# K's later rests and copies queued behind a unit, the first weight conversions spaced out, layer 2's blocks split one block further ahead

## Chip, core and metric

One Trainium2 chip, one core. The metric is the device time of one execution in microseconds (us): the median over several runs. Everything runs on the five engines of that core: TensorE (PE in the rows, with PEld for its weight loads), VectorE (DVE), ScalarE (ACT), GpSimd (POOL) and SyncE (SP, which here only issues DMAs).

## What is computed

Three stages follow one another; the output of each is the input of the next.

```python
# attention: 2 batches, 8 heads, 768 rows, 64 columns a head
q_bucket, k_bucket = hash6(q @ proj), hash6(k @ proj)      # 6 sign bits each
scores = where(q_bucket == k_bucket, scale * q @ k.T, -1e9)
attn = softmax(scores) @ v
x = attn as 1536 tokens x 512
x = (silu(x @ w_gate) * (x @ w_val)) @ w_out              # layer 1, 512 -> 1536 -> 512
h = x @ w_in                                              # layer 2, 512 -> 2048 -> 512
out = (max(h, 0) + alpha * min(h, 0)) @ w_out2
```

## The kernel before

**Attention.** Two heads make a pair, four pairs make the 512 columns of a token. An item is one pair with 256 query rows, a unit is one head of an item. The items run in a fixed order: items 0 to 7 are the four pairs with the first 512 query rows (items 0 and 1 are pair 0, 2 and 3 pair 1, 4 and 5 pair 2, 6 and 7 pair 3), and the rest follow. A unit passes through `banks` (three score tiles S, a copy `se` of each on ACT, running maxima `m` on DVE), `top` (transposes `mt` on PE, row maximum `mq` on DVE), `back` (transposes `mb`, the subtraction `s_sub` of L333 on DVE, the exponential `s_exp` of L338 on ACT) and `values` (matmuls `po`, then the division on DVE, a rounded copy `xh` on ACT and its rest `xl` on POOL). Eight steps of the generator `attention()` make a unit. Several units are in flight, a stage apart.

**K of a pair.** Products run in a reduced format on PE, so an operand is held as a rounded part and a rest. For K of a pair, `load_k` (L165) loads the plain rows into `nat`, on SP, and the rounded part into the tile `kt`, on POOL's queue. `rest_k` (L177) subtracts the two: head 0 on POOL, head 1 on DVE. `copy_k` (L181) copies the rounded part to a second half on ACT, once per head. Then `hash_k` makes the hash rows from both (matmuls `hp`, `mk` on DVE, L210 on ACT). For items 2, 4 and 6 these calls stand in `prep`, which is written two items ahead of its use.

**Weights.** A block is 128 x 512. Its raw 64-bit words are loaded (`raw_load`, L560), converted to one float (`w_conv`, which calls `round64`: L585 on ACT, L586 and L588 on DVE, L590 on POOL), split into a rounded part (`w_h`, L625, ACT) and a rest (`w_l`, L632, POOL or DVE in turn), and used. The tag `raw64` has two buffers, and K's `nat` and the raw blocks share them. Converted blocks have three buffers (`wt`), split blocks four (`wb`) in layer 1 and six (`wb2`) in layer 2. `prime(k)` (L838), called after each step k of the attention that runs alone at the start, loads the first seven blocks and converts the first four. `w_ahead(n)` (L644) does the same for all later blocks, as far ahead of block n as `LEAD[0]` (layer 1) or `LEAD[1]` (layer 2) says.

**What sets the order.** The kernel's text is traced in program order, and a planner then sets the order of each engine's queue with its own estimates of durations: at each moment it takes, of the instructions that it holds to be ready, the one that stands first in the text. An instruction may therefore be queued far ahead of its place. On the chip each engine takes its queue strictly in that order, and waits where an operand is late. `keep_in_program_order` (in `pin`) forbids the moving ahead: the instruction stays behind the one that stands before it in the text on the same engine. The conversions' first instructions and the raw loads are pinned in this way, K's rests and copies are not.

**Phases.** The attention of items 0 to 7 runs alone, up to about 125 us. Then layer 1 of tokens 0 to 511 and of 512 to 1023 runs with the rest of the attention woven in (to about 450 us), layer 1 of the last 512 tokens follows (to about 585 us), and layer 2 of all tokens ends the kernel. During the first pass of layer 2 its last blocks are still loaded and converted (`w_late`), and `ws.late` keeps all of `w_l` on DVE.

Of the kernel before, what the change touches and what calls it, by code (L numbers as in the profile page):

```python
# [12 lines left out]
AF = mybir.ActivationFunctionType  # L13
ALU = mybir.AluOpType
# [8 lines left out]
RAWB = 2  # L23
WB = (3, 4, 6)

LEAD = ((2, 2, 3, 5), (3, 4, 5, 7))

PL = (2, 1)

# [6 lines left out]

POOL_K = (1, 0)

PRIME = (64, 6)

MANY = 14

# [12 lines left out]
def lsh_attention_moe_kernel(  # L55
# [12 lines left out]
    nc = tc.nc  # L68
    B, H, D, S = qT.shape
# [3 lines left out]
    P = 128  # L73
# [15 lines left out]
    def f32(ap):  # L89
        return ap.bitcast(F32)  # L90
# [37 lines left out]
    def setup_alpha():  # L128
        nc.sync.dma_start(out=al, in_=alpha)
# [5 lines left out]
    at = Bag()  # L135

    def KA(it):
        return KT[it.p][:, 0:2, :]

    def KB(it):  # L140
        return KT[it.p][:, 2:4, :]
# [34 lines left out]

    def rest_k(it, x, eng):  # L177
        a = KA(it)[:, x, :]
        eng.tensor_tensor(out=a[D:P], in0=it.nat[x * D:(x + 1) * D, :], in1=f32(a)[0:D], op=ALU.subtract)

    def copy_k(it, x):  # L181
        nc.scalar.activation(out=KB(it)[0:D, x, :], in_=f32(KA(it))[0:D, x, :], func=AF.Copy)

    def round_q(it):
        it.QA = at.sm.tile([P, 2, GQ], F32R, tag="QA", name="QA", bufs=2)
# [44 lines left out]
    def prep(it):  # L230

        def rest():
            pass

        todo = []
        if it.first and it.b == 0:
            todo += [lambda x=x: rest_k(it, x, nc.gpsimd if POOL_K[x] else nc.vector) for x in range(2)]
            todo += [lambda x=x: copy_k(it, x) for x in range(2)]
        if it.first and it.b > 0:
            todo += [lambda: load_v(it)]  # L240
        todo += [lambda: round_q(it), lambda: rest_q(it)] + [rest] * (8 if at.alone else 4)
        if it.first and it.b == 0:
            todo += hash_k(it, 0) + hash_k(it, 1)
        todo += hash_q(it)
        last = todo[-1]

        def end():
            last()
            it.ready = True

        todo[-1] = end
        return todo

    def prep_k(it):
        todo = [lambda x=x: rest_k(it, x, nc.gpsimd if POOL_K[x] else nc.vector) for x in range(2)]
        todo += [lambda x=x: copy_k(it, x) for x in range(2)]
        return todo + hash_k(it, 0) + hash_k(it, 1)
# [14 lines left out]
    def first_item(it):  # L272
        ka, kb = KA(it), KB(it)
        for x in range(2):
            nc.scalar.activation(out=ka[0:D, x], in_=it.nat[x * D:(x + 1) * D, :], func=AF.Copy)
        round_q(it)
        for x in range(2):
            rest_k(it, x, nc.vector)
        nc.vector.tensor_tensor(out=it.QB[0:D], in0=it.qr[0:D], in1=f32(it.QA)[0:D], op=ALU.subtract)
        for x in range(2):  # L280
            nc.scalar.activation(out=kb[0:D, x], in_=it.nat[x * D:(x + 1) * D, :], func=AF.Copy)
        for fn in hash_q(it) + hash_k(it, 0, "G") + hash_k(it, 1, "G"):
            fn()
        it.ready = True
# [45 lines left out]

    def s_sub(u):

        nc.vector.scalar_tensor_tensor(  # L333
            out=u.se, in0=u.se, scalar=FLOOR, in1=u.mx[:, None, :].to_broadcast([P, NC, GQ]),
            op0=ALU.max, op1=ALU.subtract)

    def s_exp(u):
        ins = nc.scalar.activation(out=u.se, in_=u.se, func=AF.Exp, scale=SCALE)  # L338
        if not at.alone:
            tc.keep_in_program_order(ins)  # L340

# [39 lines left out]
    for b in range(B):  # L381
# [3 lines left out]
        for p, g in order:  # L385
            it = Bag()
# [2 lines left out]
            it.first = not any((o.b, o.p) == (b, p) for o in items)  # L389
            items.append(it)  # L390
    at.done = 0
    at.alone = True
    at.halves = True

    def attention():
# [37 lines left out]
        def release():  # L433
            while held:
                s_exp(held.pop(0))
# [27 lines left out]
        def back(u):  # L463
            s_mb(u)
            s_sub(u)
            held.append(u)
            if at.alone:
                release()
            step()
            yield  # L470
# [167 lines left out]
    def upto(name, n, fn):  # L638
        n = min(n, NWT)
        while getattr(ws, name) < n:  # L640
            fn(getattr(ws, name))
            setattr(ws, name, getattr(ws, name) + 1)

    def w_ahead(n):  # L644

        lead = LEAD[n >= NW1]
        for name, k, fn in (("load", 2, w_load), ("conv", 1, w_conv), ("h", 0, w_h)):
# [190 lines left out]
    def prime(k):  # L838

        if k == 60:  # L840
            setup_alpha()
        k -= PRIME[0]
        if k >= 0 and k % PRIME[1] == 0:
            i = k // PRIME[1]
            upto("load", min(i, 7), w_load)
            if i >= 4:
                upto("conv", min(i - 3, 4), w_conv)

    k = 0
    per = NPAIR * (W // GQ)  # L850
    while at.done < per:
        at.alone = at.done < per - 2
        more()
        k += 1
        prime(k)
# [103 lines left out]
```

## Time and profile before

| what | us |
|---|---|
| median of 3 runs (852.6 to 853.44) | 853.03 |
| the profiled execution | 854.37 |
| its span, first to last instruction | 852.5 |
| PE busy in it | 816.9 (96%) |
| DVE busy | 539.4 (63%) |
| ACT busy | 442.4 (52%) |
| POOL busy | 349.6 (41%) |

The shares are means over stages with different limits, so the stretches below are read one by one.

### The profile page before, as it was taken

How to read it: one execution, taken by the hardware profiler on the slowest of the kernel's cores; microseconds unless marked ns; L12 is line 12 of the kernel's file. 1: busy time of each engine (PE TensorE's matmuls, PEld its weight loads, DVE VectorE, ACT ScalarE, POOL GpSimd, SP SyncE). 2: the span in 40 equal slices, each digit the busy share in tenths (PEclk: the TensorE clock that was granted, in tenths of full speed). 3: DMA queues.
4: the chain of work that ended last, by engine and by line, in shares of the span. 5: the costliest groups of instructions: out<-in, count | busy, mean ns of one | idle time of the engine just before them, and what ended most of it. 6: DMA issues, size and time to landing. Idle time of an engine off the chain costs nothing.

```text
span 852.5 us, 11166 instructions
## 1 busy us (share of the span) xinstructions
PE 816.9 (96%) x3988; PEld 683.0 (80%) x3988; DVE 539.4 (63%) x825; ACT 442.4 (52%) x738; POOL 349.6 (41%) x285
## 2 busy tenths in 40 slices
PE   5899789899999999999999999999999999999998
PEld 3788678687778888888888888887788888888886
DVE  6778988898887875665664342347977443334332
ACT  7887786877676755555543232224433333333331
POOL 6212426575655632322321342433442354435441
PEclk9999999999999999999999999999999999999999
DMA  9220536776756547554545687875500300010001
GB/s 236 45 75 28 170 113 209 222 230 195 257 205 219 180 156 275 167 192 173 175 148 185 234 269 238 264 265 174 173 0 1 149 1 0 1 50 1 0 1 50
DMA packets 57287, 122.03 MB, mean 143 GB/s; under 512 B 16912, under 2 KB 29200, under 8 KB 56720
## 3 DMA queue, kind: packets, MB, share of 16 engines
q1 hardware_dynamic: 56080, 118.51, 42.4%
q0 software_dynamic: 1008, 2.75, 1.5%
q8 instruction: 32, 0.52, 0.2%
q14 instruction: 23, 0.19, 0.1%
q10 hardware_dynamic: 144, 0.05, 0.0%
HBM read 94.03 MB, written 27.26 MB: 142 GB/s over the span
## 4 chain that ended last, share of the span: by engine, by line
PE 69%; DVE 12%; DMA 7%; ACT 5%; issue 4%; POOL 1%; SPq 0%; DVEq 0%; ACTq 0%; POOLq 0%
PE po L348 9%; PE gp L690 8%; PE gp L689 8%; PE gp L688 8%; PE op L694 5%; PE op L695 5%; PE op L693 5%; PE hp L688 5%; PE hp L690 5%; PE hp L689 5%; DMA raw<-in_wblk_dram 4%; PE S L296 2%; PE S L297 2%; DVE wt L588 2%; DVE wt L586 2%
## 5 line engine op out<-in xcount | busy, mean ns | idle before, releaser
L683 POOL TENSOR_TENSOR gl<-ex,gh 128x512 fp32r<-128x512 f32 x81 | 109.1, 1347 | 187.4 <-ACT gh L680 170.0
L348 PE MATMUL po<-se,vv 128*128 128x256 f32 x576 | 140.8, 384 | 5.7 <-ACT se L338 3.3
L348 PEld LDWEIGHTS po<-se,vv 128*128 128x128 f32 x576 | 107.0, 191 | 24.0 <-ACT se L338 5.7
L680 ACT ACTIVATE gh<-ex 128x512 fp32r<-128x512 f32 x84 | 53.1, 632 | 134.5 <-DVE ex L677 85.2
L688 PE MATMUL gp<-xh,wb 128*128 128x512 f32 x288 | 120.6, 419 | 0.5 <-ACT xh L373 0.5
L690 PE MATMUL gp<-xh,wb 128*128 128x512 f32 x288 | 113.4, 394 | 0.0
L689 PE MATMUL gp<-xl,wb 128*128 128x512 f32 x288 | 113.2, 393 | 0.0
L590 POOL TENSOR_TENSOR wt<-wt,wr 128x512 int32<-128x512 int32 x48 | 64.3, 1344 | 84.8 <-DVE wt L588 39.0
L625 ACT ACTIVATE wb<-w 128x512 fp32r<-128x512 f32 x96 | 59.3, 627 | 70.6 <-PE hp L690 56.0
L674 DVE TENSOR_SCALAR ex<-hp,al 128x512 f32<-128x512 f32 x48 | 35.9, 747 | 92.4 <-PE hp L690 91.1
L298 ACT ACTIVATE se<-S 128x512 f32<-128x512 f32 x144 | 81.6, 592 | 23.2 <-PE S L297 20.6
L296 PE MATMUL S<-QA,kt 128*128 128x256 f32 x288 | 80.6, 306 | 9.5 <-ACT se L298 4.6
L333 DVE SCALAR_TENSOR_TENSOR se<-se,mb 128x1536 f32<-128x1536 f32 x48 | 83.6, 1741 | 1.9 <-PE mb L328 1.8
L694 PE MATMUL op<-wb,gh 128*128 128x512 f32 x192 | 74.8, 390 | 1.8 <-DVE wb L632 1.8
L338 ACT ACTIVATE se<-se 128x1536 f32<-128x1536 f32 x48 | 71.2, 1482 | 8.9 <-DVE se L333 8.7
L297 PE MATMUL S<-qb,kt 76*128 76x256 f32 x288 | 74.3, 286 | 0.8 <-ACT kt L210 0.8
L695 PE MATMUL op<-wb,gl 128*128 128x512 f32 x192 | 74.7, 389 | 0.0
L688 PE MATMUL hp<-xh,wb 128*128 128x512 f32 x192 | 74.7, 389 | 0.0
L689 PE MATMUL hp<-xl,wb 128*128 128x512 f32 x192 | 74.7, 389 | 0.0
L690 PE MATMUL hp<-xh,wb 128*128 128x512 f32 x192 | 74.7, 389 | 0.0
L693 PE MATMUL op<-wb,gh 128*128 128x512 f32 x192 | 74.7, 389 | 0.0
L296 PEld LDWEIGHTS S<-QA,kt 128*128 128x128 f32 x288 | 54.6, 190 | 17.4 <-ACT se L298 7.2
(99 smaller groups left out, 1672.4 us busy)
## 6 DMA issues: line engine op xcount, KB each, us to landing
wb<-w SPq DMA_DIRECT2D x72, 512.0 KB, 4.1
raw<-in_wblk_dram SPq DMA_DIRECT2D x68, 512.0 KB, 4.4
w<-wb SPq DMA_DIRECT2D x36, 512.0 KB, 3.0
qr<-in_q_dram SPq DMA_DIRECT2D x24, 256.0 KB, 2.8
nat<-in_k_dram SPq DMA_DIRECT2D x8, 384.0 KB, 3.3
vv<-in_v_dram SPq DMA_DIRECT2D x16, 192.0 KB, 4.4
whole<-wt SPq DMA_DIRECT2D x12, 256.0 KB, 2.2
w<-whole SPq DMA_DIRECT2D x12, 256.0 KB, 4.3
```

The lines of the kernel that those rows point to most:

```text
L296: nc.tensor.matmul(pt[:, i, :], lhsT=ka[:, sl], rhs=qa, start=True, stop=False)
L297: nc.tensor.matmul(pt[:, i, :], lhsT=kb[:, sl], rhs=qb, start=False, stop=True)
L298: nc.scalar.activation(out=u.se[:, 2 * j:2 * j + 2, :], in_=pt, func=AF.Copy)
L333: nc.vector.scalar_tensor_tensor(out=u.se, in0=u.se, scalar=FLOOR, in1=u.mx[:, None, :].to_broadcast([P, NC, GQ]), op0=ALU.max, op1=ALU.su ...
L348: nc.tensor.matmul(it.po[:, u.x, :], lhsT=VV[it.b, it.p][:, kb, u.x * D:u.x * D + P], rhs=u.se[:, kb, :], start=kb == 0, stop=kb == NC - 1)
L683: eng.tensor_tensor(out=l, in0=ex, in1=f32(h), op=ALU.subtract)
L688: nc.tensor.matmul(pt, lhsT=h, rhs=ah, start=first, stop=False)
L689: nc.tensor.matmul(pt, lhsT=h, rhs=al_, start=False, stop=False)
L690: nc.tensor.matmul(pt, lhsT=l, rhs=ah, start=False, stop=last)
L693: nc.tensor.matmul(pt, lhsT=gh, rhs=h, start=first, stop=False)
L694: nc.tensor.matmul(pt, lhsT=gh, rhs=l, start=False, stop=False)
L695: nc.tensor.matmul(pt, lhsT=gl, rhs=h, start=False, stop=last)
```

## The change

Three things are edited.

- `rest_k` on DVE and `copy_k` on ACT of items 4 and 6 get an order-only edge: on their engine they may not be queued before the second last subtraction (for the rest) or exponential (for the copies) that stands ahead of them in the text. A step writes these calls for item 4 when units 0 to 3 have been subtracted, for item 6 when units 0 to 6 have been (its copies when unit 7 has too).
- `PRIME` goes from (64, 6) to (36, 16). Before, raw blocks 0, 1, 2, ... are loaded after steps 70, 76, 82, ... and blocks 0 to 3 converted after steps 88, 94, 100 and 106. Now blocks 0 and 1 are loaded after step 36 and one more after each of steps 52, 68, 84, 100 and 116, and blocks 0 to 3 are converted after steps 52, 68, 84 and 100, each time ahead of the load. Sixteen steps are two units.
- `LEAD[1]` goes from (3, 4, 5, 7) to (4, 5, 5, 7): when block n of layer 2 is taken, rounded parts are written up to block n + 4 (n + 3 before) and rests up to block n + 3 (n + 2 before). Loads and conversions reach as far as before.

```diff
-LEAD = ((2, 2, 3, 5), (3, 4, 5, 7))
+LEAD = ((2, 2, 3, 5), (4, 5, 5, 7))
...
-PRIME = (64, 6)
+PRIME = (36, 16)
...
     def rest_k(it, x, eng):
         a = KA(it)[:, x, :]
-        eng.tensor_tensor(out=a[D:P], in0=it.nat[x * D:(x + 1) * D, :], in1=f32(a)[0:D], op=ALU.subtract)
+        ins = eng.tensor_tensor(out=a[D:P], in0=it.nat[x * D:(x + 1) * D, :], in1=f32(a)[0:D], op=ALU.subtract)
+        if eng is nc.vector:
+            behind(it, ins, at.subs)
+
+    def behind(it, ins, old):
+        if 4 <= it.i < 8 and len(old) >= 2:
+            tc.add_manual_dep(ins.ins, old[-2], mybir.DependencyInfo(
+                mybir.DependencyClass.NoSync, mybir.DependencyReason.DATA), reason="a later pair")
 
     def copy_k(it, x):
-        nc.scalar.activation(out=KB(it)[0:D, x, :], in_=f32(KA(it))[0:D, x, :], func=AF.Copy)
+        ins = nc.scalar.activation(out=KB(it)[0:D, x, :], in_=f32(KA(it))[0:D, x, :], func=AF.Copy)
+        behind(it, ins, at.exps)
...
+        at.subs.append(ins.ins.name)
...
+        at.exps.append(ins.ins.name)
...
+    at.subs, at.exps = [], []
...
-            upto("load", min(i, 7), w_load)
-            if i >= 4:
-                upto("conv", min(i - 3, 4), w_conv)
+            upto("conv", min(i, 4), w_conv)
+            upto("load", min(i + RAWB, 7), w_load)
```

## Rows read from the trace of the kernel before

**Rows 1.** Busy time of each engine by stretch: length, busy (instructions), clock, DMA share, GB/s.

```profile
55.00:82.00 27.00, 25.39 (x158) 22.07 (x157) 21.59 (x34) 22.92 (x38) 4.43 (x5) 1.00 0.20 69
82.00:106.00 24.00, 19.67 (x106) 16.38 (x106) 23.52 (x35) 18.54 (x32) 11.70 (x10) 0.93 0.46 154
...
125.00:300.00 175.00, 166.40 (x852) 139.46 (x851) 150.57 (x238) 126.36 (x215) 109.15 (x84) 0.99 0.66 212
...
585.00:620.00 35.00, 33.23 (x147) 27.18 (x147) 33.57 (x43) 15.89 (x28) 17.82 (x13) 1.00 0.47 166
620.00:845.00 225.00, 225.00 (x994) 186.40 (x993) 100.28 (x140) 78.19 (x127) 97.58 (x76) 1.00 0.05 19
```

**Rows 2.** Chain of waits, in order of time: start, length, what.

```profile
16.11 7.29 DMA nat<-in_k_dram
...
26.83 0.63 PE mt L316 x4
...
90.23 2.30 DVE wt L586
...
98.57 0.74 POOL wb L632
...
108.64 0.56 ACT wr L585
...
144.79 3.08 DMA nat<-in_k_dram
```

**Rows 3.** Timeline of DVE, 10 to 60 us: start, length, instruction, idle time before it.

```profile
16.48 0.95 DVE L179 TENSOR_TENSOR kt<-nat,kt 64x768 fp32r<-64x768 f32 x1
...
23.50 0.95 DVE L179 TENSOR_TENSOR kt<-nat,kt 64x768 fp32r<-64x768 f32 x1 [1.84 <-DMA nat<-in_k_dram]
...
29.99 1.74 DVE L333 SCALAR_TENSOR_TENSOR se<-se,mb 128x1536 f32<-128x1536 f32 x1
...
35.33 0.69 DVE L317 TENSOR_REDUCE mq<-mt 128x2 f32<-128x512 f32 x1 [2.24 <-PE mt L316]
...
53.73 1.74 DVE L333 SCALAR_TENSOR_TENSOR se<-se,mb 128x1536 f32<-128x1536 f32 x1
```

**Rows 4.** Timeline of ACT, 10 to 60 us.

```profile
20.00 0.83 ACT L182 ACTIVATE kt<-kt 64x768 fp32r<-64x768 f32 x1
...
24.27 2.31 ACT L182 ACTIVATE kt<-kt 64x768 fp32r<-64x768 f32 x3
```

**Rows 5.** All of L586, 60 to 130 us: count, shortest/median/longest in ns.

```profile
L586 DVE TENSOR_SCALAR wt<-raw x7: 375/416/2303, 82.3 to 127.9; 128x512 int32<-128x512 int32 x7
```

**Rows 6.** Timeline of DVE, 60 to 85 us.

```profile
62.11 0.69 DVE L317 TENSOR_REDUCE mq<-mt 128x2 f32<-128x512 f32 x1 [1.80 <-PE mt L316]
...
63.08 1.72 DVE L333 SCALAR_TENSOR_TENSOR se<-se,mb 128x1536 f32<-128x1536 f32 x1
...
76.70 1.74 DVE L333 SCALAR_TENSOR_TENSOR se<-se,mb 128x1536 f32<-128x1536 f32 x1
...
80.15 0.48 DVE L204 TENSOR_SCALAR mk<-hp,cq 44x256 f32<-44x256 f32 x1 [1.10 <-PE hp L199]
...
83.20 0.68 DVE L588 SCALAR_TENSOR_TENSOR wt<-raw,wt 128x512 int32<-128x512 int32 x1
```

**Rows 7.** Timeline of POOL, 60 to 85 us.

```profile
64.22 1.29 POOL L190 TENSOR_TENSOR qb<-qr,QA 64x512 fp32r<-64x512 f32 x1 [8.81 <-ACT QA L187]
...
78.16 1.27 POOL L190 TENSOR_TENSOR qb<-qr,QA 64x512 fp32r<-64x512 f32 x1 [1.78 <-ACT QA L187]
```

**Rows 8.** Timeline of PE, 88 to 108 us.

```profile
88.03 2.86 PE L348 MATMUL po<-se,vv 128*128 128x256 f32 x12 [0.46 <-ACT se L338]
...
102.94 4.03 PE L348 MATMUL po<-se,vv 128*128 128x256 f32 x12
```

**Rows 9.** Layer 2's beginning: L632 on DVE, 590 to 640 us, and who waited for it.

```profile
L632 DVE TENSOR_TENSOR wb<-w,wb x19: 674/1109/1773, 596.7 to 639.6; 128x512 fp32r<-128x512 f32 x19
...
PE op L694: 1.8, 1
```

More of the change, by code (lines that the diff above doesn't have):

```diff
@@ L331, in s_sub @@
     def s_sub(u):
-        nc.vector.scalar_tensor_tensor(
+        ins = nc.vector.scalar_tensor_tensor(
             out=u.se, in0=u.se, scalar=FLOOR, in1=u.mx[:, None, :].to_broadcast([P, NC, GQ]),
             op0=ALU.max, op1=ALU.subtract)
+        at.subs.append(ins.ins.name)
     def s_exp(u):
         ins = nc.scalar.activation(out=u.se, in_=u.se, func=AF.Exp, scale=SCALE)
+        at.exps.append(ins.ins.name)
         if not at.alone:
```

## Prediction

> **What bounds the kernel now.** I read the busy time by stretch first [rows 1]. From 620 to 845 us PE is busy for all of its 225 us and the other engines for less than half: there nothing but PE counts. From 82 to 106 us it is the other way round: DVE is busy 23.52 of 24.00 us and PE only 19.67, where from 55 to 82 us DVE has 21.59 of 27.00 and PE 25.39. So the attention that runs alone has a stretch, the one of the first weight conversions, in which DVE sets the pace, beside one with room. From 125 to 300 us PE misses 8.6 us (175.00 less 166.40), from 585 to 620 us 1.77.
>
> Next the chain of waits [rows 2], to see what the early stretches wait for. It runs through K's load of pair 3 (16.11 us, 7.29 us long), then through a conversion on DVE (90.23, 2.30 us), a rest of a weight block on POOL (98.57, 0.74) and a conversion on ACT (108.64, 0.56). The timelines show the same places on their engines. The rest of pair 2's K stands on DVE at 16.48, that of pair 3's at 23.50 behind 1.84 us of idle time for its load [rows 3]; the copies stand on ACT at 20.00 and 24.27 (the last group is three of them, 2.31 us) [rows 4]. Pair 3's rest is written only in step 64 of the text, so the planner has queued it some 40 us ahead, and sooner than its data comes. What the early part saves should pass through: no engine waits for a clock time, and the later phases are a queue of PE work behind it.
>
> **K's rests and copies.** Removed from the early queue are two DVE instructions of 0.95 us, four ACT instructions of 0.83, and the wait of 1.84 us [rows 3, 4]. On the chain the wait and the rest behind it are 1.84 + 0.95 = 2.8 us. Not all of it need come off: PE has its own work there until shortly before the transposes at 26.83 [rows 2], so I take the wait alone, 1.8. The least is about 1.0 (one rest, 0.95), the most 2.8.
>
> What is moved comes back. Pair 2's rest now stands behind unit 2's subtraction (29.99), pair 3's behind unit 5's (53.73). Behind the one DVE idles for 2.24 us before 35.33 [rows 3], behind the other for 1.80 us before 62.11 [rows 6]; each hides 0.95, so the rests cost nothing there, and 1.9 in all without that cover. The copies follow unit 2's and unit 6's exponentials, where ACT is nearly full (22.92 of 27.00 us from 55 to 82 [rows 1]). I take one of the four as felt, 0.8 us; the ends are 0 and 4 x 0.83 = 3.3. Sum of this part: -1.8 + 0.8 = -1.0, between -2.8 and +2.3.
>
> **Conversions.** Block 0's conversion was written after step 88 and moves to after step 52, blocks 1, 2 and 3 from after 94, 100 and 106 to after 68, 84 and 100. A pinned conversion is queued behind the last DVE instruction written before it, which for the first three is the subtraction of unit 5, 7 and 9 (at 53.73, 63.08 and 76.70 [rows 3, 6]), and for block 3 that of unit 11. Gone from the stretch at 82 to 106 us are the three chain pieces, 2.30 + 0.74 + 0.56 = 3.6 us [rows 2].
>
> One conversion on DVE is 0.42 for L586 (the median) and 0.68 for L588 [rows 5, 6], 1.1 us. Block 0's falls before the 1.80 us of idle time at 62.11 and shares it with pair 3's rest (0.95): 0.2 over. Block 1's, at 64.8, has no such gap behind it, but the chain leaves DVE there for ACT and PE: I take half of its 1.1, 0.5. Block 2's, at 78.4, stands before the 1.10 us of idle time at 80.15 [rows 6]: 0. Block 3's stays where DVE is full: 1.1. With them goes a meeting with POOL. L586 took 2.30 us while POOL worked, against 0.42 [rows 5], and Q's rest runs on POOL from 64.22 to 65.51 and from 78.16 to 79.43 [rows 7], just where blocks 1 and 2 are now converted: 0.7 and 1.0 us of overlap, of which I count 0.5 as felt, since both are partly covered as before. Sum back: 0.2 + 0.5 + 0 + 1.1 + 0.5 = 2.3. The part gives -3.6 + 2.3 = -1.3; its ends are -3.6 (all hidden) and -3.6 + 4 x 1.1 + 1.7 = +2.5.
>
> The Trainium skill (SBUF — State Buffer, section Who interferes with whom) says that DVE and GpSimd share one pair of ports, and that whichever comes first holds it for its whole instruction while the other is fully blocked. The trace agrees: 2.30 us is one short L586 behind POOL instructions. By this rule alone both meetings would be felt in full, and the sum back would be 1.2 us more.
>
> **The clock.** PE pauses around 100 us, and the same twelve `po` matmuls that took 2.86 us at 88.03 take 4.03 at 102.94 [rows 8], because the mean granted clock of that stretch is 0.93 [rows 1]. It follows pauses in which PE waited for Q's hash, which waited for ACT and POOL among the conversions. With these gone I expect the lower level not to be granted there: -1.2 us. The ends are -1.2 and +1.2 (it is granted after another pause).
>
> **Loads.** Raw blocks 0 and 1 are written before pair 3's K load and share its two buffers, so block 0 takes the buffer that pair 1's K frees at about 16 us, block 1 the one of pair 2, and pair 3's K load waits until block 0 is converted, about 57 us. Alone such a load takes 3.08 us [rows 2]: landing at 60.1, with its rest allowed from 55.4. POOL then has the other head's rest, and the hash follows; I cost this at nothing, because of the 1.80 us in which DVE has nothing else at that place [rows 6]. If the load takes 7.29 us as it did at 16.11, it lands at 64.3, 4.2 us later. Queued behind the waiting rest on DVE are the row maximum at 62.11 and unit 7's subtraction, and PE waits for both. On SP nothing is late: the loads behind are Q's, needed many steps on. The later raw loads come sooner than before, and the split blocks' four buffers fill as before when layer 1 starts.
>
> **Layer 2's lead.** No instruction is added; rests of blocks stand one block further ahead. The one stall there is 1.8 us of PE for L632 [rows 9]. Its block's load keeps its place on SP, so I take 0; the ends are -1.8 and the price of the third rival.
>
> **Sum.** -1.0 - 1.3 - 1.2 + 0 = -3.5 us. Against the profiled execution (854.37, span 852.5) that is 850.9 and 849.0; the median of the runs is 1.34 below the profiled one, and from 853.03 it gives 849.5. A change of 0.2%, about what this kernel's measurement can tell, is 1.7 us.
>
> **Rivals.**
> 1. *Given back in layer 1.* From 125 to 300 us the fresh blocks are fed through two raw buffers, DMA is busy for 0.66 of the time and DVE for 150.57 of 175 us [rows 1]. If loads and DVE, not the start, set when this ends, the 3.5 us are lost there: 853.0. Against it: the feeding is paced by buffers that PE frees, so it starts earlier too.
> 2. *Pair 3's K comes late.* The landing moves from 60.1 to 64.3 and DVE and PE stand still: +4.2, hence 853.7. For it speaks that the planner already queued this rest 1.84 us too early [rows 3]; against it, that little else is being moved then (DMA share 0.20 from 55 to 82 us, [rows 1]).
> 3. *DVE becomes the bound at layer 2's start.* From 585 to 620 us DVE is busy 33.57 of 35.00 us [rows 1]. L632 lasts 0.67 us at the least and 1.77 at the most, 1.11 in the median [rows 9], by what POOL does. If the new order makes some ten of them long, that is 10 x (1.77 - 1.11) = 6.6 us, hence 849.5 + 6.6 = 856.1, slower. It decides once DVE's work for a block exceeds PE's time for one. Against it: products are used three blocks later, which covers several us.
> 4. *More comes off.* All moves are hidden: -2.8 - 3.6 - 1.2 - 1.8 = -9.4, hence 843.6 at the end.
>
> **How the numbers follow.** The forecast has 0.50, with its own range of 847.0 to 851.3 (851.3 is 0.2% faster). Rival 4, below 847.0, has 0.10. Rivals 1 and 2 have 0.12 and 0.11, both within 0.2%. Rival 3, with any other order of the planner that costs more than is gained, has 0.17. So faster is 0.60, same 0.23, slower 0.17. The range goes from 845.5 (half of rival 4 below it) to 855.0 (most of the slower cases above it), which leaves out about 0.2.
>
> **What would show it.** Right: no DVE idle time before a K rest near 22 us; rests of pairs 2 and 3 near 31 and 60; conversions near 55, 64, 77 and 88, and DVE's share from 82 to 106 us well under 0.98; no half clock before 125 us; the first layer 1 matmul 3 to 4 us earlier, and the same lead still there at 300 and 585 us. Wrong: K's load of pair 3 landing after 62 with DVE idle before its rest; L586 long at 64 or 78; the lead gone at 300 us; a longer pause of PE near 598.

## The result, and the profile after

| what | before | after |
|---|---|---|
| median of 6 runs, us | 853.24 (852.57 to 856.6) | 845.8 (843.88 to 849.65) |
| ratio, 95% interval | | 0.9908 [0.9885, 0.993] |
| profiled execution, us (span) | 854.37 (852.5) | 843.88 (842.0) |

The kernel became faster by 7.4 us in the medians and by 10.5 in the two profiled executions; forecast were 849.5 us and a gain of 3.5. The direction is right, but the gain is twice the predicted one: the time lies at the lower edge of the whole range (845.5 to 855.0) and below the forecast's own (847.0 to 851.3), where rival 4 had 0.10.

The stretches of the changed kernel (columns as in [rows 1]):

```profile
55.00:82.00 27.00, 23.35 (x140) 19.81 (x140) 24.50 (x38) 24.20 (x40) 10.83 (x8) 1.00 0.28 94
82.00:106.00 24.00, 21.52 (x134) 19.26 (x133) 22.10 (x36) 21.30 (x37) 9.24 (x9) 1.00 0.43 140
125.00:300.00 175.00, 170.07 (x879) 143.75 (x878) 148.86 (x235) 126.82 (x215) 108.32 (x83) 0.99 0.66 218
585.00:620.00 35.00, 34.05 (x151) 27.88 (x150) 33.55 (x40) 15.34 (x27) 17.26 (x14) 1.00 0.34 118
```

Against [rows 1] the first row lost 2.0 us of PE (25.39 to 23.35) and the second won 1.9 (19.67 to 21.52, with 134 matmuls instead of 106): the work was moved from the full stretch into the one with room, and it has a price there. The third row is the surprise. Behind the early part, from 125 to 300 us, PE now misses 4.9 us where it missed 8.6.

DVE's timeline of the changed kernel: both rests, the four pinned conversions, and block 4's behind them.

```profile
31.50 2.06 DVE L179 TENSOR_TENSOR kt<-nat,kt 64x768 fp32r<-64x768 f32 x1
...
53.56 0.41 DVE L597 TENSOR_SCALAR wt<-raw 128x512 int32<-128x512 int32 x1
...
60.22 0.45 DVE L374 STREAM_TRANSPOSE xf<-den 128x256 f32<-128x256 f32 x1 [0.95 <-ACT den L364]
60.69 1.77 DVE L179 TENSOR_TENSOR kt<-nat,kt 64x768 fp32r<-64x768 f32 x1
...
66.66 0.42 DVE L597 TENSOR_SCALAR wt<-raw 128x512 int32<-128x512 int32 x1
...
79.16 0.42 DVE L597 TENSOR_SCALAR wt<-raw 128x512 int32<-128x512 int32 x1
...
91.19 0.42 DVE L597 TENSOR_SCALAR wt<-raw 128x512 int32<-128x512 int32 x1
...
97.19 0.39 DVE L597 TENSOR_SCALAR wt<-raw 128x512 int32<-128x512 int32 x1
```

The places are close to the predicted ones (rests near 31 and 60, conversions near 55, 64, 77 and 88), and no conversion takes the 2.30 us of [rows 5] any more. The rests, though, take 2.06 and 1.77 us instead of 0.95. The last row matters most: block 4 is converted at 97 us, in the kernel before at 112.5:

```profile
112.52 0.42 DVE L586 TENSOR_SCALAR wt<-raw 128x512 int32<-128x512 int32 x1
```

To see where the gain comes from, I compare the start of each unit's subtraction (L333 before, L341 after) on the timelines of DVE (u4 is unit 4); the kernel before converts its first blocks between the units 10 and 12, and layer 1 begins during the units 16 to 20. Differences to the kernel before, in us, minus is earlier:

| kernel | u4 | u8 | u11 | u12 | u16 | u18 | u20 | u47 |
|---|---|---|---|---|---|---|---|---|
| after | -1.8 | +1.4 | +1.2 | -3.7 | -4.9 | -9.1 | -10.0 | -9.7 |
| p_alone | 0.0 | +2.9 | +4.3 | -1.3 | -0.6 | -6.3 | -7.2 | -7.8 |
| b_alone | -1.8 | -1.7 | -1.7 | -1.7 | -3.0 | -3.1 | -3.5 | -2.7 |
| fewer_loads | -2.1 | +1.2 | +1.0 | -4.0 | -4.0 | -5.6 | -5.1 | -2.8 |
| two_pinned | -1.9 | +3.0 | +2.8 | -2.4 | -3.3 | -7.8 | -8.5 | -9.9 |

In the changed kernel: 1.8 us from the removed wait, then 3.2 us given back while the conversions are spread (u4 to u8), 4.9 won where they stood before (u11 to u12), and another 5.1 between u16 and u20. The layer-2 beginning adds 0.8. The first layer 1 matmul stands at 119.27 instead of 124.92. Each row is one execution, with its own stretches of the lower clock: the kernel before has two, at 102 and 167 us, p_alone one at 16 to 19 us, fewer_loads three, at 117, 161 and 189 us. The row of fewer_loads therefore shows only roughly where it loses, and sizes are taken from the times.

What changes between u16 and u20 is seen in the chain of waits. Of the kernel before, 138 to 148 us:

```profile
138.32 4.75 DMA raw<-in_wblk_dram
...
143.09 0.93 DVE wt L586
```

and on its DVE, 138 to 144 us:

```profile
139.89 0.70 DVE L588 SCALAR_TENSOR_TENSOR wt<-raw,wt 128x512 int32<-128x512 int32 x1
143.09 0.92 DVE L586 TENSOR_SCALAR wt<-raw 128x512 int32<-128x512 int32 x1 [2.51 <-DMA raw<-in_wblk_dram]
```

The chain of the changed kernel at the same work, 124 to 153 us:

```profile
124.59 0.49 PE gp L699
...
136.25 0.86 PE po L358 x4
...
138.73 0.23 PE gp L700
...
139.23 0.64 ACT wb L636
...
141.88 1.94 DVE kt L179
...
153.04 5.24 DMA raw<-in_wblk_dram
```

Before, DVE stood for 2.51 us for a raw block, and with it the unit's maxima, and K's load of [rows 2] at 144.79 waited behind that block. After, the chain runs through PE alone from 124.6 to 139.0 and no DMA stands on it there; a raw block is on it again at 153.04. What PE loses is read from its busy time, from u16 to u18 and from u18 to u20 (columns as in [rows 1]). Before:

```profile
122.40:146.80 24.40, 23.90 (x123) 20.14 (x122) 21.72 (x33) 18.54 (x32) 14.98 (x12) 1.00 0.58 172
146.80:171.50 24.70, 21.26 (x102) 16.81 (x101) 20.97 (x35) 18.45 (x32) 14.49 (x13) 0.93 0.75 221
```

and after:

```profile
117.50:137.70 20.20, 19.67 (x106) 16.58 (x105) 17.24 (x28) 16.87 (x28) 12.91 (x10) 1.00 0.60 196
137.70:161.50 23.80, 23.48 (x124) 19.91 (x122) 20.41 (x34) 18.87 (x32) 15.07 (x14) 1.00 0.72 221
```

In the stretch of DVE's wait PE idles 0.5 us in both kernels, so the wait holds up nothing on PE there. In the next one PE idles 3.4 us before and 0.3 after. Of the 5.1 us, 3.1 are thus idle time of PE that is gone. The other 2.0 are busy time, and in it lies a stretch at a granted clock of 0.52 in this execution of the kernel before (167.0 to 170.5 us, an estimated 3.5 x 0.48 = 1.7 us).

SP's queue shows what moved. Its rows of raw blocks and of K in the changed kernel, up to 134 us:

```profile
15.14 0.40 SPq L579 DMA_DIRECT2D raw<-in_wblk_dram  x1
...
33.59 0.34 SPq L579 DMA_DIRECT2D raw<-in_wblk_dram  x1
...
55.42 0.34 SPq L168 DMA_DIRECT2D nat<-in_k_dram  x1
...
62.55 0.33 SPq L579 DMA_DIRECT2D raw<-in_wblk_dram  x1
...
70.16 0.41 SPq L579 DMA_DIRECT2D raw<-in_wblk_dram  x1
...
81.11 0.33 SPq L579 DMA_DIRECT2D raw<-in_wblk_dram  x1
...
92.78 5.91 SPq L579 DMA_DIRECT2D raw<-in_wblk_dram  x2
...
116.06 0.33 SPq L168 DMA_DIRECT2D nat<-in_k_dram  x1
122.34 1.33 SPq L579 DMA_DIRECT2D raw<-in_wblk_dram  x2
...
132.58 0.33 SPq L579 DMA_DIRECT2D raw<-in_wblk_dram  x1
133.18 0.33 SPq L168 DMA_DIRECT2D nat<-in_k_dram  x1
```

and of the kernel before its fourth to tenth raw block:

```profile
93.89 2.38 SPq L568 DMA_DIRECT2D raw<-in_wblk_dram  x2
...
102.82 0.33 SPq L568 DMA_DIRECT2D raw<-in_wblk_dram  x1
...
120.19 0.33 SPq L568 DMA_DIRECT2D raw<-in_wblk_dram  x1
...
129.32 0.33 SPq L568 DMA_DIRECT2D raw<-in_wblk_dram  x1
...
138.32 0.37 SPq L568 DMA_DIRECT2D raw<-in_wblk_dram  x1
...
140.61 0.33 SPq L568 DMA_DIRECT2D raw<-in_wblk_dram  x1
```

Seven raw blocks are on their way by 100 us (five before), the tenth at 132.58 (140.61 before), and the second K of batch 1 right behind it at 133.18, 11.6 us earlier than in [rows 2]. Both kernels name seven blocks to be loaded early. But a load needs one of two buffers, and these come free by conversions. The early spacing frees them earlier. When the first layer 1 matmul runs, both kernels hold four split blocks and have issued seven raw loads. But DVE has converted seven blocks in the changed kernel, and five, with the sixth just begun (124.63), in the kernel before. The next two raw loads stand within 4.4 us of that matmul after, and 4.4 and 13.4 us behind it before.

### The profile page after: what moved, and what is told of

Read it like the earlier page. It is cut to its first block, busy times and chain, and to the rows that moved or that the text cites. A ratio compares the mean times of both kernels' runs of the same rounds, so it can differ in the third digit from the quotient of the medians.

```text
span 842.0 us, 11156 instructions
## 1 busy us (share of the span) xinstructions
PE 813.0 (97%) x3988; PEld 681.7 (81%) x3988; DVE 536.6 (64%) x826; ACT 442.7 (53%) x738; POOL 347.5 (41%) x284
## 4 chain that ended last, share of the span: by engine, by line
PE 70%; DVE 9%; DMA 7%; ACT 7%; issue 4%; POOL 1%; SPq 0%; DVEq 0%; ACTq 0%; POOLq 0%
PE po L358 9%; PE gp L699 8%; PE gp L701 8%; PE gp L700 8%; PE op L705 5%; PE op L706 5%; PE op L704 5%; DMA raw<-in_wblk_dram 5%; PE hp L700 5%; PE hp L699 5%; PE hp L701 5%; PE S L304 2%; PE S L305 2%; ACT se L306 2%; DVE wt L599 1%
## 5 line engine op out<-in xcount | busy, mean ns | idle before, releaser
L341 DVE SCALAR_TENSOR_TENSOR se<-se,mb 128x1536 f32<-128x1536 f32 x48 | 83.5, 1740 | 3.4 <-PE mb L336 3.4
L643 DVE TENSOR_TENSOR wb<-w,wb 128x512 fp32r<-128x512 f32 x65 | 56.1, 866 | 17.4 <-ACT wb L636 17.4
```

Source lines behind the costliest of these rows:

```text
L341: ins = nc.vector.scalar_tensor_tensor(out=u.se, in0=u.se, scalar=FLOOR, in1=u.mx[:, None, :].to_broadcast([P, NC, GQ]), op0=ALU.max, op1= ...
```

## The experiments

Executions of one kernel differ here by up to 1% (850.90 to 859.68 us for the kernel before in one group of 29), and much of it goes with the granted clock. Over the 201 timed runs of all kernels a straight line with one slope and a level for each kernel gives 0.62 (standard error 0.05) us per 0.001 of a run's mean granted clock. Where a few us decide, I give the difference to the kernel before at a common clock too, with a standard error, from that line; for the change itself it is -7.4 ± 0.6. The errors leave out that the kernel before itself differs by up to 1.2 us between the three groups in which the other kernels were timed.

**The parts alone.** p_alone has only the new order of loads and conversions, b_alone only the order-only edges, l_alone only the lead, and pb the first two together.

```diff
p_alone: kernel before with
-PRIME = (64, 6)
+PRIME = (36, 16)
-            upto("load", min(i, 7), w_load)
-            if i >= 4:
-                upto("conv", min(i - 3, 4), w_conv)
+            upto("conv", min(i, 4), w_conv)
+            upto("load", min(i + RAWB, 7), w_load)
b_alone: kernel before with behind(it, ins, ...) in rest_k and copy_k
l_alone: kernel before with
-LEAD = ((2, 2, 3, 5), (3, 4, 5, 7))
+LEAD = ((2, 2, 3, 5), (4, 5, 5, 7))
pb: kernel after without the line of l_alone
```

> Only the new spacing of the first loads and conversions; K's order and layer 2's lead as before. Theory A (the spacing carries the gain, since pair 3's load then waits for a raw buffer anyway and its rest leaves the early queue without any edge): 5 to 8 us faster than before, with the long DVE conversion near 90 us gone and the lead already there when layer 1 is under way. Rival (K's order carries it): 2 us faster at most. Rival (both are needed): 1 to 3 us faster.

> Only the edges on K's rests and copies of pairs 2 and 3. Theory A: the 1.84 us wait of DVE near 22 us is gone, 1 to 2 us are gained by unit 5 and mostly given back where the rests and copies now stand, so 0 to 1.5 us faster at the end. Rival (K's order carries it): 4 to 6 us faster.

> Only layer 2's lead. All theories: up to 590 us nothing changes; the stall of 1.77 us near 598 us falls to about 0.95, so 0.8 us faster, or nothing that the runs can tell.

> Spacing and K's order together, layer 2's lead as before, that is the changed kernel without its third part. Theory A: 6 to 8 us faster than before, 0.8 us slower than the changed kernel. If the parts add up, the sum of the runs with one part alone; if both are needed, clearly more than that sum.

| kernel | median, us (before) | ratio | at a common clock |
|---|---|---|---|
| p_alone | 847.83 (854.23) | 0.9935 [0.9913, 0.9956] | -5.1 ± 0.5 |
| b_alone | 853.92 (854.23) | 0.9995 [0.9974, 1.0016] | -0.9 ± 0.5 |
| l_alone | 855.19 (854.23) | 1.0003 [0.9981, 1.0024] | +0.6 ± 0.5 |
| pb | 845.84 (854.23) | 0.9902 [0.9872, 0.9932] | -7.0 ± 0.6 |

The spacing of the loads and conversions carries most of it, and the lead nothing that the times show. p_alone and b_alone add up to -6.0 against -7.0 of both together, which the errors allow. p_alone loses the wait of 1.84 us too: pair 3's load stands behind a raw block there, and its rest moves to 62.58 us without any edge. Its execution is at 0.0 at u4 all the same; it has the half clock at 16 to 19 us and is 1.3 us late at u0. From u4 on the table of units shows two pieces inside p_alone: -1.3 at u12 and -0.6 at u16, where the net of the conversions was forecast at -1.3, and then -5.7 more from u16 to u18, which was not predicted. In b_alone the 1.8 us won stay whole through u12.

The lead is not shown to do what it was meant for. In l_alone and in the changed kernel PE waits half as long at layer 2's start (of the changed kernel, who waits for L643, 580 to 640 us; L632 in [rows 9]):

```profile
L643 DVE TENSOR_TENSOR wb<-w,wb x24: 673/898/1772, 586.2 to 639.2; 128x512 fp32r<-128x512 f32 x24
...
  PE op L705: 0.9, 1
```

That is 0.9 us where 1.8 stood, too little for the times to tell. But the same pause is 1.6 to 2.7 us in the six other kernels that have the lead, and 0.95 to 1.6 us in the five others that lack it (put_last, pb, b_alone, cluster_early, p_alone). So the shorter pause can't be put down to the lead.

**Fewer raw blocks early.** If the gain at layer 1's beginning comes from blocks that are loaded and converted ahead, it must go when fewer of them are pinned in the early part.

```diff
fewer_loads: kernel after with
-            upto("load", min(i + RAWB, 7), w_load)
+            upto("load", min(i + RAWB, 4), w_load)
```

> The changed kernel with the early loads stopped at four blocks: blocks 0 to 3 are loaded and converted after the same steps, blocks 4 to 6 are loaded only when layer 1 begins. Theory A (the second half of the gain, some 4 to 5 us between 120 and 165 us, comes from raw blocks and conversions that run further ahead when layer 1 begins): the units up to the 16th stand as in the changed kernel, the lead over before shrinks by 3 to 5 us behind them. Rival (it comes from the earlier start and the clock alone): the lead stays within 1 us of the changed kernel's.

Measured: 850.55 against 854.49, ratio 0.9964 [0.9947, 0.9982], at a common clock -3.8 ± 0.5. The early part is that of the changed kernel (-4.0 at u12). Of the 5.1 us between u16 and u20, 1.1 are left, and another 2.3 go by u47, in an execution with three stretches of the lower clock. When layer 1 starts, DVE has converted five blocks, as in the kernel before, and not seven. On SP the sixth raw block now comes at 107.25 us (raw blocks and K alone):

```profile
69.91 0.41 SPq L579 DMA_DIRECT2D raw<-in_wblk_dram  x1
...
80.87 0.33 SPq L168 DMA_DIRECT2D nat<-in_k_dram  x1
...
92.53 0.33 SPq L579 DMA_DIRECT2D raw<-in_wblk_dram  x1
...
107.25 0.33 SPq L579 DMA_DIRECT2D raw<-in_wblk_dram  x1
```

because K of batch 1, no longer held back by pinned loads, takes one of the two shared buffers at 80.87 and holds it until its rest:

```profile
114.29 0.95 DVE L179 TENSOR_TENSOR kt<-nat,kt 64x768 fp32r<-64x768 f32 x1 [1.09 <-DMA kt<-in_k_dram]
```

So three loads are worth 7.4 - 3.8 = 3.6 ± 0.8 us. k3_first (below), timed in the same group as this kernel, gives 7.2 - 3.8 = 3.4. An early K alone brings nothing: here it is 35 us earlier than in the changed kernel.

**Other stocks of raw blocks.** Three more kernels vary how much stands ready (each + line stands in place of the line of its kind). The fourth, cluster_early, keeps the close spacing of before and starts it two units earlier.

```diff
two_pinned: kernel after with
+            upto("conv", min(i, 2), w_conv)
+            upto("load", min(i + RAWB, 4), w_load)
more_ahead: kernel after with
+            upto("conv", min(i, 6), w_conv)
+            upto("load", min(i + RAWB, 9), w_load)
denser_ahead: as more_ahead, and
+PRIME = (36, 12)
cluster_early: kernel before with
+PRIME = (48, 6)
```

> The changed kernel with only blocks 0 and 1 converted and only blocks 0 to 3 loaded in the attention that runs alone; the later ones are written with layer 1, where nothing pins them, so the planner moves them ahead as it likes. Theory (raw blocks that come late at layer 1 cost 3 to 5 us): if the fifth to eighth raw block land as late as with fewer loads, the time is that kernel's, 4 us faster than before; if the planner brings them forward, the changed kernel's.

> The changed kernel with the same spacing of sixteen steps, up to six blocks converted and nine loaded, so that the fifth and sixth conversion are pinned behind steps 116 and 132. Theory: they come later than the planner puts them in the changed kernel (97 and 109 us), so nothing is gained, and up to 3 us may be lost. Rival (more blocks pinned ahead, more gain): 1 us or more faster than the changed kernel.

> The changed kernel with twelve steps between loads instead of sixteen, and with up to six blocks converted and nine loaded before layer 1. Theory: more blocks stand ready, but the four buffers of split blocks bound it, and DVE is fuller from 55 to 90 us: within 2 us of the changed kernel. Rival (every block more gains again): 2 us or more faster than it.

> The kernel before with its dense conversions moved forward as they are: loads after steps 54, 60, ..., conversions after steps 72, 78, 84 and 90 instead of 88 to 106. Theory (both the spacing and the blocks that stand ready count): the dense stretch only moves to 65 to 90 us and DVE is as full there, the fifth and sixth block are converted at most a little earlier, so 0 to 2 us faster than before. Rival (what counts is that they are early): 4 us faster or more.

| kernel | median, us (before) | ratio | at a common clock | 10th raw block / 2nd K of batch 1 loaded at |
|---|---|---|---|---|
| two_pinned | 847.12 (853.27) | 0.9933 [0.9911, 0.9954] | -6.1 ± 0.5 | 133.80 / 134.40 |
| more_ahead | 846.38 (853.27) | 0.992 [0.9899, 0.9941] | -7.1 ± 0.6 | 133.23 / 135.33 |
| denser_ahead | 850.81 (853.27) | 0.9976 [0.9959, 0.9993] | -1.6 ± 0.5 | 138.75 / 142.62 |
| cluster_early | 851.85 (853.27) | 0.9983 [0.9966, 1.0] | -3.1 ± 0.5 | 134.91 / 138.51 |
| fewer_loads | 850.55 (854.49) | 0.9964 [0.9947, 0.9982] | -3.8 ± 0.5 | 136.04 / 139.22 |

The first row corrects me. two_pinned pins as few loads as fewer_loads and its K comes as early (81.25), yet it keeps most of the gain: the conversions of blocks 2 and 3 are left to the planner, which frees the buffers sooner, and the next raw blocks load at 87.57 and 98.56 instead of 92.53 and 107.25. So it is not the number of pinned loads but when the buffers come free. more_ahead shows that no more is to be had: two blocks more in stock give nothing. denser_ahead missed its expectation of 2 us from the changed kernel. It has nine blocks on their way by 113.43 us (more_ahead by 128.21) and keeps the least: it stands at +5.5 at u11 for its closer conversions, and its raw blocks then keep K of batch 1 out of the shared buffers, whose two loads come only at 136.72 and 142.62, with the tenth block between them. cluster_early has -1.0 at u8, loses 4.2 to u11, at its cluster and with a half clock at 80 to 83 us, and wins 2.8 from u16 to u18. A larger stock has a price, in spacing and in buffers that K wants too.

PE's idle time from u18 to u20 goes with the gain in most of these kernels. It is 3.5 us in b_alone, 3.6 in l_alone, 3.4 in cluster_early and 2.3 in fewer_loads, where 3.4 stood before; it is 0.9 in p_alone, 0.6 in two_pinned and 0.3 in pb and k3_first. denser_ahead lies between with 1.6, and more_ahead, with 2.5, does not fit.

**Does pair 3's K come late?** The second rival.

```diff
k3_first: kernel after with
-            upto("load", min(i + RAWB, 7), w_load)
+            upto("load", min(i + 1, 7), w_load)
```

> The changed kernel with one raw block loaded after step 36 instead of two, and each later one a block later, so that pair 3's K is loaded near 33 us and not behind the first conversion near 55 us. Theory: pair 3's rest on DVE then meets no rest of the same pair on POOL and lasts 0.95 us instead of 1.77, so 0.8 us are gained between units 5 and 8, and the raw blocks are no later when layer 1 begins: within 1 us of the changed kernel. Rival (pair 3's late load is what gives back 3 us between units 5 and 8): 2 to 3 us faster there.

Measured: 845.77 against 854.49, ratio 0.9903 [0.9877, 0.9929], at a common clock -7.2 ± 0.6: the same as the change. Pair 3's K is loaded at 34.92 us instead of 55.42, and its rest takes 0.95 us again instead of 1.77:

```profile
62.02 0.95 DVE L179 TENSOR_TENSOR kt<-nat,kt 64x768 fp32r<-64x768 f32 x1
```

The 0.8 us won there had been lost at the start, where this execution is 1.3 us later than the changed kernel's at u4; it has a half clock at 16 to 19 us. The rival is refuted: what the late load costs is the 0.8 us of a longer rest, not 4.2.

**Is it the put behind which the raw load stands?** Before the wait of 2.51 us, the late raw load followed the copying of a split block on SP. I moved those copies behind the loads, in the kernel before and in the changed one.

```diff
put_last: kernel before, in w_ahead (both places; after_put_last: kernel after)
-        upto("put", n + 1, w_put)
...
+        upto("put", n + 1, w_put)
```

> The kernel before, in which a split block is written back to memory behind the loads of the same call instead of ahead of them, so that a raw load does not queue on SP behind a write that waits for a rest. Nothing else is changed. Theory A (the 2.51 us in which DVE waits for a raw block at 143 us come from that queue): up to 120 us nothing changes, the wait is gone, 2 to 3 us faster than before. Rival (the raw load waits for a buffer, not for the queue): the same time as before.

> The changed kernel with the same edit of the write back. If the raw loads already run ahead of the writes there (theory A), no difference from the changed kernel beyond 1 us; if SP's queue is a cost of its own, 2 us faster than the changed kernel.

put_last: 859.45 against 854.49, ratio 1.0077 [1.0048, 1.0105]. after_put_last: 850.8, ratio 0.9962 [0.994, 0.9983]. Both are misses. The edit did not reach the place: the raw load of 138.32 still stood at 137.24, and up to 150 us the order was as before. At a common clock put_last is 4.8 ± 0.6 us slower than the kernel before and after_put_last 3.4 ± 0.8 slower than the changed one, so the copies must not be late. They decide nothing on the theory: whether the raw load of 138.32 would have come sooner without the copy ahead of it, issued at 137.89, stays open.

## Why the prediction was right or wrong

**K's rests and copies: right in the wait, not in what comes back.** Forecast -1.0 from -1.8 and +0.8, with -1.8 at u4 in the trace of b_alone and -0.9 ± 0.5 in its times. The removed wait is the whole of the 1.8, as taken. The 0.8 for a copy on ACT did not show in b_alone (still -1.7 at u12), so the nearness of -0.9 to -1.0 owes something to luck. The cover of the rests held on DVE (0.95 us of idle time before 60.22, where 1.80 stood), but their length was wrong. Pair 2's now meets Q's rest on POOL (31.48 to 32.75), pair 3's the other head's (59.83 to 61.65):

```profile
31.48 1.27 POOL L198 TENSOR_TENSOR qb<-qr,QA 64x512 fp32r<-64x512 f32 x1 [9.96 <-ACT QA L195]
...
59.83 1.82 POOL L179 TENSOR_TENSOR kt<-nat,kt 64x768 fp32r<-64x768 f32 x1
```

Both times DVE's rest ends 0.81 us after POOL's instruction, that is about one rest of 0.95 later: it stood still while POOL worked. The Trainium skill (SBUF — State Buffer, section Who interferes with whom) says that a DVE instruction with two inputs in SBUF contends with a GpSimd instruction that reads SBUF, and that this is an exclusive lock. The trace agrees with the 0.81: POOL's instruction had begun first both times. I had applied this to the conversions, which were spared, and not to the rests.

**Conversions: right in the early part.** Forecast -3.6 + 2.3 = -1.3; p_alone stands at -1.3 at u12, the changed kernel at -1.9 beside the 1.8 of the wait. Both sides were larger, in p_alone +4.3 up to u11 and -5.6 from u11 to u12, so the net owes something to luck. One of the three pieces was also misread: the 0.56 us at 108.64 lies outside the stretch and is the sixth conversion on ACT, not one of the four that moved. And DVE stayed fuller than expected there, 22.10 of 24.00 us (0.92, where well under 0.98 was forecast).

**The clock: a size about right, an argument that does not hold.** The mean granted clock of the timed runs went from 0.9952 to 0.9963, which by the line is -0.7 ± 0.5 us (forecast -1.2), and the stretch from 82 to 106 us has 1.00 instead of 0.93. What the lower clock there costs is seen in b_alone, whose execution lacks it: -1.7 at u13, -3.2 at u14. But the pauses that I blamed are not enough: b_alone has pauses of PE of 1.63 us at 91.7 and 1.04 at 100.6 like the kernel before, and no drop behind them:

```profile
98.00:102.00 4.00, 2.44 (x15) 1.92 (x15) 3.96 (x9) 3.68 (x6) 2.07 (x2) 1.00 0.38 138
102.00:106.00 4.00, 3.86 (x28) 3.45 (x26) 2.91 (x5) 3.09 (x7) 1.21 (x2) 1.00 0.50 189
```

And the changed kernel has a drop elsewhere (below).

**Loads: the step that failed.** "The later raw loads come sooner than before, and the split blocks' four buffers fill as before when layer 1 starts." Both halves came true: in both kernels four blocks are split when layer 1 starts, the last rest at 104.03 us (112.86 before). What failed is the price of zero that I drew from them, because the stock does not end with the split blocks. Blocks 4 to 6 are converted at 97, 109 and 116 us where it was 112.5, 124.6 and 127.9, so more converted blocks stand behind the four, the raw buffers come free sooner, and the second K of batch 1 is loaded 13.9 us after the first layer 1 matmul instead of 19.9. PE's idle time from u18 to u20 falls from 3.4 to 0.3 us. In the times this is worth -3.6 ± 0.8 us by fewer_loads, which makes up most of the difference between -3.5 and -7.4. The row that would have told it was one that I quoted, K's load on the chain at 144.79 [rows 2]: I did not ask what it had waited for.

**Layer 2's lead: right in the times.** Forecast 0, measured +0.6 ± 0.5 alone. The 0.8 us less pause of PE in the changed kernel is inside the ends given, but the other kernels do not show it to come from the lead.

**The sum.** In the two profiled executions: -1.8 and -1.9 up to u12, about -1.2 up to u16 (where the kernel before has its lower clock), -5.1 up to u20, +0.3 to the end of the attention, -0.8 at layer 2: -10.5 together. At a common clock the change is -7.4 on average; of the 3.1 us between, 1.2 to 1.7 are the second stretch of the lower clock that the one execution of before has ahead of PE's last matmul (below), and the rest is what one execution differs from another. The terms from the traces are good to that and no better.

**The rivals.** The first (given back from 125 to 300 us) came out with the other sign. The second fell with k3_first. The third did not happen: PE's pause at layer 2 is 0.95 us in the changed kernel, not longer than 1.8. The fourth, more comes off, is the direction, but by a mechanism that it did not name; its own -9.4 had moves hidden that the traces show to be felt.

**What stays open.** DVE's wait for the raw block does not idle PE where it stands. How much of the 3.6 us comes by it later, through the order of PE's work and K's load, and how much is conversions that have left the stretch from 125 to 150 us, was not separated. The load time of the second K goes with u20 over these kernels, but it stands behind the raw blocks on one queue and can be a mark rather than a cause.

## What to carry to other kernels

A prefetch that is begun earlier and spread out can be worth more where its consumer starts than where it was moved from: ask what stock stands ready at that moment, and follow each DMA on the chain back to what freed its buffer. Buffers shared by two streams are the thing to count, in order of time, on the queue that issues them. Price the spacing too, since a larger stock bought with denser work on a full engine lost nearly all of the gain.

## What the runs showed of the hardware that was not expected

Stretches of the lower clock come at differing places in kernels whose pauses are alike. Of the kernel before, at 102 and 167 us (PE's pauses are 1.61 us before 93.41, 1.04 before 102.27 and 1.97 before 165.84; b_alone, with the same two early ones, has no drop there):

```profile
102.00:105.50 3.50, 3.23 (x10) 2.62 (x11) 3.42 (x6) 2.28 (x5) 1.80 (x3) 0.51 0.63 204
...
167.00:170.50 3.50, 3.50 (x12) 2.82 (x11) 2.19 (x4) 3.30 (x7) 1.40 (x2) 0.52 0.79 299
```

Of the changed kernel, at 195 us, behind pauses of PE of 1.37 us before 192.53 and 0.92 before 194.19:

```profile
195.00:198.40 3.40, 3.40 (x12) 2.71 (x11) 1.53 (x4) 3.32 (x7) 1.69 (x3) 0.52 0.94 343
```

About half of the full clock is the 1.2 GHz level. One such stretch in a run of 850 us is worth about 0.002 of its mean clock, 1.2 us by the line above, and runs of one kernel differ by several of them (cluster_early's twelve runs have mean clocks of 0.988 to 0.998).
